# A spectral mixing layer with its dense DFT matmuls replaced by a factored FFT kept in SBUF

## The chip, the cores and the metric

One core of a Trainium2 chip. The metric is the device time of one execution in microseconds (us); where several runs are given, it is their median with the lowest and highest. Runs of one comparison are made on one chip, alternating with the kernel before. Engines: PE is TensorE, PEld its weight loads, DVE is VectorE, ACT is ScalarE, POOL is GpSimd, SP issues the transfers. "Granted clock" is the share of full speed that TensorE was given. The record calls a run slow when it is over 1.5% above the fastest run of the same kernel, and fast otherwise; its verdicts (faster, same or slower by 2%, or unclear) use fast runs alone.

## The reference, cut to what matters

```python
def _A_ref(x, w_r, w_i):                    # x: (1, 2048, 512) bf16
    X = jnp.fft.rfft2(x.astype(jnp.float32), axes=(-2, -1))
    X = X * (w_r + 1j * w_i)                # (2048, 257) spectral weights
    return jnp.fft.irfft2(X, s=(S, D), axes=(-2, -1)).astype(jnp.bfloat16)

h  = x + _A_ref(_layernorm(x), w_r, w_i)
# FFN: 512 -> 1792, squared ReLU, -> 512
r  = jnp.maximum(_layernorm(h) @ w1 + b1, 0)
h2 = h + (r * r) @ w2 + b2
```

## The kernel before

The transforms over rows (2048) and channels (512) are dense matmuls with tables of cosines and sines. They use the fold of row t with row 2048-t, which needs reversed copies of x. Everything is 128-partition bf16, accumulated in PSUM in f32.

```python
for q, (sk, szk) in enumerate(kcols):              # forward transform over rows
    prs = [ps_tile(f"par{db}") for db in range(ND)]
    for c in range(NT):
        for db in range(ND):
            nc.tensor.matmul(prs[db][:, 0:szk], lhsT=xe[:, c, bass.ts(db, P)],
                             rhs=FC[:, c, sk:sk + szk], start=(c == 0), stop=False)
# ... the same with sine tables (pai), then channels (pxr, pxi), z_batch on VectorE,
# ... then the inverse over rows (pcp, psm)

def d2_tile(j):                                    # inverse over channels, residual, statistics
    # ... 4 + 4 matmuls into pyc and pys
    nc.scalar.copy(ysn[:], pys[:, 0:D])
    nc.vector.tensor_tensor(ylo[:], pyc[:, 0:D], ysn[:], ALU.add)
    nc.vector.tensor_tensor(yhi[:], pyc[:, 0:D], ysn[:], ALU.subtract)
    nc.vector.tensor_tensor(xn[:, j, :], xn[:, j, :], ylo[:], ALU.add)
    nc.vector.tensor_tensor(xrv[:, j, :], xrv[:, j, :], yhi[:], ALU.add)
    # ... bn_stats and bn_aggr of both

for g in gorder:                                   # FFN, four groups of 512 rows
    # ... normalise, transpose into UT
    for i in range(NF):                            # NF = 14
        for cd in range(ND):                       # ND = 4
            nc.tensor.matmul(ph[:], lhsT=W1[:, cd, bass.ts(i, P)], rhs=UT[:, g, cd, :], ...)
        nc.scalar.activation(rl[:], ph[:], ACT.Relu, bias=b1f[:, i:i + 1], scale=1.0)
        nc.vector.tensor_tensor(actT[:, i, :], rl[:], rl[:], ALU.mult)
    for ii in range(4):
        for f_i in range(NF):
            nc.tensor.matmul(po[:, 0:D], lhsT=actT[:, f_i, bass.ts(ii, P)], rhs=W2[:, f_i, :], ...)
        nc.tensor.matmul(po[:, 0:D], lhsT=onesrow[0:1, :], rhs=b2b[0:1, :], start=False, stop=True)
        # ... residual, for half of the rows a reversal matmul, store
```

## Time and profile before

| | before |
|---|---|
| time, 3 runs known ahead | 285.85 us (285.51 to 287.39) |
| span of the profiled run | 284.6 us |
| TensorE busy / idle in the span | 232.0 / 52.6 us |
| mean granted clock | 0.94 |

The prediction shows the lines on which it rests. One more view, the span in 40 equal slices of 7.1 us, gives the whole picture of TensorE: the first row is its busy share in tenths, the second the granted clock in tenths.

```profile
PE   0040497999999997999996059999999899999994
...
PEclk9995597989999999999999659999999999999999
```

The 9s from the eighth slice on say that TensorE is nearly always busy and at full clock. The two weak places are the first 35 us and the three slices around 160 us (6, 0, 5).

### The profile page before, as it was taken

The page shows a single profiled execution, that of the slowest core. Times are in us where ns is not written, and L with a number is a line of the kernel's source. Part 1 is how long each engine was busy: PE and PEld are TensorE (multiplying, and loading weights), DVE is VectorE, ACT ScalarE, POOL GpSimd, SP SyncE. Part 2 cuts the span into 40 slices and gives each one's busy share as a digit, 9 for nine tenths or more (in the row PEclk, how much of TensorE's full clock was granted, in tenths as well). Part 3 has the DMA queues.
Part 4 walks back from the last instruction along what each step waited for, and adds up shares of the span by engine and source line. Part 5 has one row for each costly group of instructions (what it writes and reads, how often), then busy time and mean ns, then how long its engine had stood idle before and what let it go on. Part 6 is the DMA issues. An engine that isn't in the chain of part 4 may idle for free.

```text
span 284.6 us, 3080 instructions
## 1 busy us (share of the span) xinstructions
PE 232.0 (81%) x1108; PEld 99.9 (35%) x1108; DVE 140.5 (49%) x317; ACT 131.5 (46%) x205; POOL 49.0 (17%) x62
## 2 busy tenths in 40 slices
PE   0040497999999997999996059999999899999994
PEld 0010133444444443444442034434443444444431
DVE  5278956482301999319909963411531143225310
ACT  1098969967633320232234068702841485048311
POOL 8237699883200000000000000000000000000000
PEclk9995597989999999999999659999999999999999
DMA  5474890000000000000000000011000100110011
GB/s 148 125 184 108 267 277 0 3 0 1 2 0 0 0 3 0 0 0 2 0 0 0 0 0 3 0 37 37 3 0 32 44 0 0 37 39 0 0 37 38
DMA packets 13097, 10.17 MB, mean 36 GB/s; under 512 B 2585, under 2 KB 12570, under 8 KB 13082
## 3 DMA queue, kind: packets, MB, share of 16 engines
q1 hardware_dynamic: 13082, 9.98, 12.1%
q8 instruction: 8, 0.13, 0.2%
q14 instruction: 7, 0.06, 0.1%
HBM read 7.88 MB, written 2.10 MB: 35 GB/s over the span
## 4 chain that ended last, share of the span: by engine, by line
PE 62%; DVE 17%; ACT 9%; POOL 5%; DMA 3%; issue 2%; SPq 1%; DVEq 0%; ACTq 0%
PE ph L444 18%; PE po L453 17%; PE pai L214 5%; PE psm L339 5%; POOL gen_i L20 5%; PE pcp L330 3%; DMA Gx<-in_A_x_dram 3%; DVE gen_m L22 2%; PE po L455 2%; DVE bnst2e L390 2%; PE pyc L371 2%; PE pxr L296 2%; PE pxr L294 2%; ACT xrv L121 1%; PE pys L375 1%
## 5 line engine op out<-in xcount | busy, mean ns | idle before, releaser
L453 PE MATMUL po<-W,actT 128*128 128x512 bf16 x224 | 52.1, 380 | 0.0
L444 PE MATMUL ph<-UT,W 128*128 128x512 bf16 x224 | 50.7, 386 | 0.7 <-ACT UT L439 0.7
L20 POOL TENSOR_SCALAR gen_i<-idx_i,tcols 128x1025 int32<-128x1025 int32 (+1 forms) x30 | 41.9, 1406 | 18.0 <-DVE mv L156 11.9
L448 DVE TENSOR_TENSOR actT<-rl 128x512 bf16<-128x512 bf16 x56 | 23.8, 426 | 34.3 <-ACT rl L447 34.0
L447 ACT ACTIVATE rl<-ph,b1f 128x512 bf16<-128x512 f32 x56 | 36.9, 692 | 8.0 <-PE ph L444 7.8
L196 PE MATMUL par<-FC,xe 128*128 128x512 bf16 (+1 forms) x96 | 18.7, 346 | 17.2 <-DVE xe L172 14.6
L444 PEld LDWEIGHTS <-W 128*128 128x128 bf16 x224 | 22.2, 99 | 28.1 <-issue 3.9
L453 PEld LDWEIGHTS <-actT 128*128 128x128 bf16 x224 | 20.9, 98 | 25.6 <-issue 2.7
L22 DVE TENSOR_SCALAR gen_m<-gen_i 128x1025 int32<-128x1025 int32 (+1 forms) x30 | 19.4, 652 | 13.7 <-POOL gen_i L20 9.4
L439 ACT COPY UT<-putp 128x512 bf16<-128x512 bf16 x16 | 8.2, 598 | 26.6 <-PE putp L438 26.6
L196 PEld LDWEIGHTS <-xe 128*128 128x128 bf16 x96 | 7.8, 104 | 28.8 <-DVE xe L172 15.5
L330 PE MATMUL pcp<-FC,PT 128*128 128x512 bf16 (+1 forms) x72 | 16.7, 379 | 1.2 <-DVE PT L277 1.2
L465 ACT CAST orv<-prout 128x512 bf16<-128x512 f32 x8 | 4.7, 585 | 26.2 <-PE prout L463 22.3
L457 DVE TENSOR_TENSOR ot<-po,xrv 128x512 bf16<-128x512 f32 x8 | 5.5, 692 | 22.2 <-PE po L455 22.2
L457 DVE TENSOR_TENSOR ot<-po,xn 128x512 bf16<-128x512 f32 x8 | 5.5, 692 | 20.9 <-PE po L455 20.9
L214 PE MATMUL pai<-FS,xo 128*128 128x512 bf16 x64 | 15.8, 411 | 0.0
L438 PE MATMUL putp<-ident,u 128*128 128x128 bf16 x64 | 5.3, 242 | 12.5 <-DVE u L429 12.2
L120 PE MATMUL prx<-Gx,Rm 128*128 128x512 bf16 x8 | 3.6, 625 | 14.1 <-DMA Gx<-in_A_x_dram 14.1
L339 PE MATMUL psm<-FS,MT 128*128 128x512 bf16 x64 | 14.3, 379 | 0.0
L332 ACT CAST CPT<-pcp 128x512 bf16<-128x512 f32 x8 | 4.2, 596 | 19.1 <-DVE bufB L262 10.2
L23 ACT ACTIVATE FS<-gen_m,biascol 128x1025 bf16<-128x1025 int32 x9 | 10.2, 1157 | 2.3 <-DVE gen_m L22 2.2
L23 ACT ACTIVATE FC<-gen_m,biascol 128x1025 bf16<-128x1025 int32 x9 | 10.0, 1145 | 2.0 <-DVE gen_m L22 1.9
(141 smaller groups left out, 288.6 us busy)
## 6 DMA issues: line engine op xcount, KB each, us to landing
W<-in_B_w_dram SPq DMA_DIRECT2D x2, 1792.0 KB, 12.5
xn<-in_A_x_dram SPq DMA_DIRECT2D x8, 128.0 KB, 2.3
out_dram<-ot SPq DMA_DIRECT2D x8, 128.0 KB, 1.7
Gx<-in_A_x_dram SPq DMA_DIRECT2D x7, 128.0 KB, 6.3
out_dram<-orv SPq DMA_DIRECT2D x7, 128.0 KB, 2.8
WLr<-in_A_w_r_dram SPq DMA_DIRECT2D x1, 514.0 KB, 3.9
WLi<-in_A_w_i_dram SPq DMA_DIRECT2D x1, 514.0 KB, 5.2
Gw<-in_A_w_r_dram SPq DMA_DIRECT2D x7, 64.2 KB, 3.3
```

Of the source, the lines that this page charges most:

```text
L20: nc.gpsimd.tensor_scalar(fi[:], idx_i_ap, col_f, float(add_const), ALU.mult, ALU.add)
L22: nc.vector.tensor_single_scalar(fm[:], fi[:], period - 1, ALU.bitwise_and)
L23: nc.scalar.activation(out_ap, fm[:], ACT.Sin, bias=biascol, scale=2.0 * np.pi / period * (1.0 - delta))
L196: nc.tensor.matmul(prs[db][:, 0:szk], lhsT=xe[:, c, bass.ts(db, P)], rhs=FC[:, c, sk:sk + szk], start=(c == 0), stop=False)
L214: nc.tensor.matmul(pis[db][:, 0:szk], lhsT=xo[:, c, bass.ts(db, P)], rhs=FS[:, c, sk:sk + szk], start=(c == 0), stop=(c == NT - 1))
L330: nc.tensor.matmul(pcs[b][:, 0:szs], lhsT=lhs, rhs=rhs, start=(c == 0), stop=(c == NT))
L339: nc.tensor.matmul(pms[b][:, 0:szs], lhsT=MT[:, c, bass.ts(b, P)], rhs=FS[:, c, ss:ss + szs], start=(c == 0), stop=(c == NT - 1))
L444: nc.tensor.matmul(ph[:], lhsT=W1[:, cd, bass.ts(i, P)], rhs=UT[:, g, cd, :], start=(cd == 0), stop=(cd == ND - 1))
L447: nc.scalar.activation(rl[:], ph[:], ACT.Relu, bias=b1f[:, i:i + 1], scale=1.0)
L448: nc.vector.tensor_tensor(actT[:, i, :], rl[:], rl[:], ALU.mult)
L453: nc.tensor.matmul(po[:, 0:D], lhsT=actT[:, f_i, bass.ts(ii, P)], rhs=W2[:, f_i, :], start=(f_i == 0), stop=False)
L457: nc.vector.tensor_tensor(ot[:], po[:, 0:D], h_tile(i), ALU.add)
```

## The change

The intent: a radix split of both transforms. Rows are 16 x 128, so a row transform is a small 16-point stage, a twiddle folded into tables, and a 128-point stage. Channels are handled as real 2 x 256. The transform's arithmetic falls from some 464 wide matmuls to about 97,000 columns in small ones, the reversed copies of x go, and what lies between the layer norm and the FFN stays in SBUF. The work is now a loop over eight pairs of row frequencies (stages 2 to 4), then a "prep" of each group of four row blocks (stages 5 and 6, residual, statistics, normalising, transposing) ahead of the FFN ("MLP") of that group. The diff is 824 lines; this is its core.

```diff
-        for q, (sk, szk) in enumerate(kcols):
-            ...                                     # dense row DFT, 8 x 4 matmuls of 512 per chunk
+    for pr in range(8):
+        pu = mm_tile("p2")                          # stage 2: 8 matmuls of 256 columns
+        ...
+        U = fwd.tile([P, 2, 512], BF16, tag="U", bufs=2, name="U")
+        nc.scalar.copy(U[:].rearrange("p q c -> p (q c)"), pu[:])
+        px = mm_tile("p3")                          # stage 3: 4 matmuls of 512
+        ...
+            nc.scalar.copy(AB[:].rearrange("p u r c -> p (u r c)"), px[:])
+            nc.vector.tensor_tensor(Xf[:, 0::3], AB[:, 0], bsw, ALU.add)
+            nc.vector.tensor_tensor(Xf[:, 2:0:-1], AB[:, 0], bsw, ALU.subtract)
+        for m, w in ((mA, WB[0]), (mB, WB[1])):     # spectral weights
+            nc.vector.tensor_tensor(m[:], X[:], w[:, pr]..., ALU.mult)
+        ...                                         # Z (2 instructions), M (2)
+        pt = mm_tile("p4")                          # stage 4: 8 matmuls of 256
+        ...
+        nc.scalar.copy(T2[:, :, :, 2 * pr:2 * pr + 2, :]..., pt[:]...)
@@
+    def prep(c):
+        for g in range(4 * c, 4 * c + 4):
+            ...                                     # stage 5: 4 matmuls of 256 into pe
+            nc.scalar.copy(od[:], pe[:, 256:512])
+            nc.vector.tensor_tensor(R[:, 0:256], pe[:, 0:256], od[:], ALU.add)
+            nc.vector.tensor_tensor(R[:, 256:512], pe[:, 0:256], od[:], ALU.subtract)
+            py = bank("p6")
+            nc.tensor.matmul(py[:], lhsT=KI[:], rhs=R[:], start=True, stop=True)
+            nc.vector.tensor_tensor(hs[:, g, :], py[:], xs[:, g, :], ALU.add)
+            ...                                     # bn_stats, bn_aggr
+            nc.gpsimd.tensor_tensor(hb[:, g, :], hs[:, g, :], b2b[:], ALU.add)
+        nc.gpsimd.tensor_scalar(rs2[:, sl], mv2[:, sl, 1], EPS, None, ALU.add)
+        nc.gpsimd.tensor_tensor(rs2[:, sl], rs2[:, sl], mhalf[:], ALU.pow)
+        ...                                         # normalise, transpose into UT
@@
-                nc.tensor.matmul(po[:, 0:D], lhsT=onesrow[0:1, :], rhs=b2b[0:1, :], start=False, stop=True)
...
+            nc.vector.tensor_tensor(ot[:], po[:], hb[:, g, :], ALU.add)
@@
+    prep(0)
+    prep(1)
+    mlp(0)
+    prep(2)
+    mlp(1)
+    prep(3)
+    mlp(2)
+    mlp(3)
```

## The prediction

> **What bounds the kernel now.** I read the page's first part, then the table of stretches, then the chain in order of time, then the groups of instructions for unit costs.
>
> ```profile
> PE 232.0 (81%) x1108; PEld 99.9 (35%) x1108; DVE 140.5 (49%) x317; ACT 131.5 (46%) x205; POOL 49.0 (17%) x62
> ```
>
> TensorE is busy for 232 of 284.6 us. The stretches (start:end, length, busy us and count of PE, PEld, DVE, ACT, POOL, granted clock, DMA share, GB/s) show where:
>
> ```profile
> 14.00:35.00 21.00, 6.22 (x15) 2.03 (x16) 17.54 (x47) 19.48 (x26) 11.37 (x7) 0.68 0.65 178
> 60.00:93.00 33.00, 32.35 (x152) 14.51 (x150) 9.54 (x25) 17.16 (x34) 6.98 (x10) 1.00 0.00 1
> 160.00:168.00 8.00, 1.41 (x12) 1.00 (x13) 7.45 (x23) 1.88 (x4) 0.00 (x0) 0.50 0.00 0
> 175.00:284.60 109.60, 104.38 (x500) 44.93 (x498) 33.64 (x69) 47.04 (x76) 0.00 (x0) 1.00 0.06 20
> ```
>
> To 35 us layer norm and sine tables run and PE waits. From there to 154 us PE is dense in the DFT matmuls. From 154 to 168 us VectorE finishes the statistics with PE idle at half clock. Then comes the FFN. The chain agrees: layer norm, tables, matmuls, a VectorE tail, then the FFN alone (start us, us, what):
>
> ```profile
> 27.84 1.36 DVE un L166 x2
> ...
> 55.63 15.06 PE pai L214 x61
> ...
> 139.98 7.03 PE psm L339 x32
> ...
> 164.43 0.23 DVE mv L391 x2
> ...
> 169.07 13.57 PE ph L444 x56
> 182.64 3.02 PE po L453 x14
> 185.66 0.32 PE po L455
> ```
>
> So the time is 164.4 us of transform, 4.6 us to the first FFN matmul, 111 us of FFN and 4.5 us of tail. One warm FFN matmul of 512 columns costs 50.7/224 = 0.226 us. The unit costs that I use:
>
> ```profile
> L378 ACT COPY ysn<-pys 128x512 f32<-128x512 f32 x8 | 4.7, 585 | 10.0 <-PE pys L375 4.7 <-DVE yhi L382 3.6 <-DVE bnst2e L390 1.2
> L173 DVE TENSOR_TENSOR xo<-un,urv 128x512 bf16<-128x512 bf16 x8 | 3.3, 407 | 0.0
> L272 DVE TENSOR_TENSOR bufA<-bufA,tmp 128x1028 bf16<-128x1028 bf16 x1 | 0.7, 701 | 0.0
> L381 DVE TENSOR_TENSOR ylo<-pyc,ysn 128x512 f32<-128x512 f32 x8 | 5.3, 663 | 8.6 <-ACT ysn L378 8.6
> L390 DVE BATCH_NORM_STATS2 bnst2e<-xn 128x6 f32<-128x512 bf16 x8 | 5.5, 683 | 0.0
> L20 POOL TENSOR_SCALAR gen_i<-idx_i,tcols 128x1025 int32<-128x1025 int32 x18 | 31.1, 1739 | 15.8 <-DVE mv L156 11.9 <-DVE gen_m L22 3.4
> ```
>
> Handoffs between engines take about 0.03 us in the chain. Independent VectorE instructions in a row start about 0.09 us before the one ahead ends; dependent ones do not.
>
> **What the Trainium skill says.** "TensorE: Matmul & The Clock Gate", Part 1, has TensorE at half clock after an idle window of about 3.4 us, and at full clock only after a busy one. The trace agrees: PE stops at 154.1, the clock falls to 0.50 at 158.2, and it returns at 171.9, 2.8 us into dense matmuls. One 1.9 us hole at 42.4 was enough for half clock from 45.5. The same page, Part 3, "What overlaps and what doesn't", has matmuls strictly first in, first out. This decides the change; no line of this trace contradicts it. "ScalarE: Activation LUTs", "What ACT_TABLE_LOAD costs", gives 186 ns + 0.833 ns an element: 613 ns for 512, measured 585, so I take 1.02 us for 1024 elements. "GPSIMD Engine Reference", 3.1, gives about 2.6 cycles at 1.2 GHz an element for two-input work: an estimate of 1.1 us for the new 512-wide residual add there. No trace line has one.
>
> **The change, part by part.** *Arithmetic.* The dense DFT groups (about 464 matmuls of 512 columns, with the reversals and edge columns about 130 us of PE busy time) go. In their place are, by counting columns, 64x256 (row stage), 28x128 (transposes), 14x256 (weight reversal), 8 pairs of 16x256 + 4x512, and 16 rows of 4x256 + 512: 97,000 columns. At 512 columns in 0.216 us they are 41 us, at half clock 82. If PE still set the end, about 90 us would go. But in the built order PE's queue is serial: stage 4 of pair k stands before stage 2 of pair k+1 for every pair but the first, and each "prep" group stands whole between two MLP groups. PE thus waits through every other engine's work.
>
> *Prologue, estimate 38.5 us.* x comes in four transfers; the first lands about 3.7. Layer norm needs 16 x (0.70 + 0.41 to 0.49) on VectorE, about 20 us with set-up. But each chunk's rstd is made on GpSimd, behind tables and weight scaling in its queue: two scalings of 2048 elements at 1.1 ns (undisturbed) to 1.7 ns (the row above) = 2.3 to 3.5 us each, also waiting for the spectral weights' DMA, and a 1152-wide table ahead of the last chunk. I work the last chunk out at 27.5. ScalarE then has that chunk's two copies (2 x 1.02) and the last E sine (1.25): 32.5. Transposes need all three E kinds, 28 x 0.12 = 3.4, then the reversal matmuls 14 x 0.213 = 3.0 at half clock: 38.9, say 38.5.
>
> *Pair loop, 83 us.* One period is: stage 4 and the next stage 2, 15 x 0.213 + 0.40 = 3.6; U copy 1.02; stage 3, 3 x 0.427 + 0.61 = 1.9; copy 1.02; VectorE 0.32 + 0.41 + 0.60 + 0.69 + 0.32 + 0.41 + 0.32 + 0.41 = 3.5; handoffs 0.15. That is 11.2 us at half clock and 9.0 at full. VectorE's 3.5 with its copy leaves PE idle over 4.5 us per period, more than a clock window, so I expect mostly half clock: 10.6. Seven periods 74, the first pair 11, less the missing last stage 2 and the hoisted part of pair 1 (3), plus the last copy 1: 83. The small real-channel fixes on GpSimd lie beside four stage-4 matmuls that do not need them.
>
> *Preps, 60 us.* One row block runs stage 5, 3 x 0.213 + 0.40 = 1.04; od copy 0.37; sum and difference from PSUM (half of 0.663's slope) 0.79 with an aggregate between; stage 6, 0.61; then the residual and statistics beside the next stage 5. That is 2.9 us per block cold and 2.7 warm. A group of four is 1.4 + 3 x 2.9 + 3.0 = 13.1, then rstd on GpSimd 0.8, normalising 1.5, and transposes 1.1 to 1.4. Two groups before the first MLP are 30; the other two, each exposed between MLPs, 15 each.
>
> *FFN, 104 us.* 4 x 112 x 0.2225 = 99.7. The bias matmul (0.32 x 16 = 5.1 us on the chain) and the reversal (8 x 0.38) are gone. Three cold starts add about 2 us each, less three early matmuls each: +4. Tail: 0.7 + a store of about 2.3 = 3.
>
> Sum: 38.5 + 83 + 60 + 104 + 3 = 288.5 of span, 289.7 with the 1.2 us by which timed runs exceed the profiled span (285.85 against 284.6). So 90 us of matmul saved come back as serial latency.
>
> **Rivals.** (1) PE stays the bound and the saving shows: 41 us of transform in place of 130, the tables smaller: about 200 us. For it: PE is 81% busy now. Against: the strict queue order, 4.5 us of other engines per pair. (2) The clock stays up in loop and preps: 1.6 less per pair and 0.2 per block give about 275. For it: stages 4 and 2 run back to back for 3.6 us, nearly a window; against: the one 1.9 us hole in the trace already cost the clock. (3) GpSimd sets the prologue: if its strided bf16 scaling or its power function runs at several times the 1.1 ns per element, the prologue becomes 45 to 50 and the total 297 to 300; no trace line has such work. (4) VectorE sets the loop: no, it has 28 us of 83.
>
> **Range and chances.** Prologue +-4, loop -14 to +7, preps -6 to +4, FFN +-2. The loop and prep errors lean towards shorter, since I took nearly cold PE and no overlap that the order does not show. I therefore place the point below the sum, at 284 us, with 268 to 299. Half of the mass is within 2% (280.1 to 291.6) or near it: faster 0.38, same 0.41, slower 0.21.
>
> **What would show it.** Right: PE busy near 60%, granted clock 0.5 to 0.65 between 40 and 150 us; eight equal periods of 10 to 11.5 us in the chain, with VectorE 3.5 of each; PE holes of some 10 us before the third and fourth MLP group; the first FFN matmul that is followed densely near 150 us. Wrong: stage 2 of pair k+1 running during VectorE's part of pair k, periods under 9 us, the prologue past 45 us, or preps hidden beside MLP matmuls.

## The result, and the profile after

| | before | after |
|---|---|---|
| time, 4 runs each, same chip | 286.53 us (285.51 to 287.39) | 294.00 us (293.55 to 294.48) |
| ratio | | 1.0249, 95% interval 1.0206 to 1.0293 |
| span of the profiled run | 284.6 us | 292.4 us |
| TensorE busy / idle | 232.0 / 52.6 us | 180.6 / 111.8 us |
| mean granted clock | 0.94 | 0.784 |

A ratio here is over fast runs alone, and not quite the ratio of the medians. The kernel became 2.5% slower, and the table says how: TensorE lost 51 us of busy time and gained 59 us of idle time.

The first part of the page of the kernel after, engines with busy time, share and count:

```profile
PE 180.6 (62%) x858; PEld 93.2 (32%) x872; DVE 128.3 (44%) x299; ACT 93.0 (32%) x123; POOL 56.7 (19%) x109
```

No engine is near full. The table of stretches of the kernel after, columns as in the prediction, cut near the first loop matmuls (they start at 41.1), at the end of the loop, and each change between prep and dense FFN matmuls:

```profile
0.00:41.50 41.50, 19.16 (x112) 12.75 (x113) 25.68 (x68) 16.43 (x17) 22.67 (x49) 0.88 0.57 194
41.50:125.10 83.60, 35.92 (x168) 20.50 (x168) 27.68 (x63) 25.98 (x27) 10.69 (x36) 0.65 0.00 0
125.10:159.20 34.10, 15.79 (x75) 8.93 (x77) 20.05 (x48) 5.26 (x11) 11.71 (x12) 0.55 0.00 1
159.20:182.80 23.60, 23.49 (x110) 10.77 (x110) 8.03 (x17) 10.66 (x16) 0.00 (x0) 1.00 0.05 17
182.80:200.20 17.40, 7.59 (x39) 4.01 (x39) 10.71 (x25) 1.89 (x5) 5.83 (x6) 0.61 0.03 8
```

TensorE idles 22.3 us of the prologue, 47.7 us of the loop (83.6 less 35.9), 37.7 us of the preps (18.3 here, 9.8 here, 9.6 in the last one). The FFN stretches, here one of four, have none. The last three are 23.5, 23.5 and 24.2 us, the last prep 17.5 and the tail 3.5. In the dense stretch TensorE runs at full clock; in loop and preps at 0.55 to 0.65.

One period of the loop, from the chain in order of time of the kernel after (start us, us, what):

```profile
86.68 1.02 ACT AB L277
87.72 0.43 DVE X L282
88.52 0.69 DVE mA L288
89.21 0.61 DVE mB L288
89.84 0.43 DVE Z L290
90.73 0.44 DVE M L300
93.23 1.39 PE p L251 x8
94.70 1.02 ACT U L254
96.96 1.02 ACT AB L277
```

From one AB copy to the next is 10.28 us. The work passes from engine to engine, each waiting for the one before, so none is busy for half of it. (Shorter pieces fall out of this list of the longest and fill its gaps: the second X, Z and M, stage 4's eight matmuls from 91.2 to 93.2, and stage 3's four from 95.8.) What TensorE waits for stands in its groups (line, engine, what, shape, count, busy us, mean ns, idle us before and its releaser); the third line is for the prologue:

```profile
L316 PE MATMUL p<-EI,M 128*128 128x256 bf16 x28 | 11.6, 414 | 32.8 <-DVE M L300 32.8
L366 PE MATMUL p<-R,KI 128*128 128x512 bf16 x16 | 8.9, 556 | 22.0 <-DVE R L364 22.0
L160 DVE TENSOR_SCALAR un<-xs,mv,rs 128x512 bf16<-128x512 bf16 x16 | 11.1, 742 | 4.7 <-POOL rs L158 4.7
```

Stage 4 waited 32.8 us for VectorE's M, 4.7 us in each of seven pairs. Stage 6 waited 22.0 us for R in the preps. In the prologue, VectorE's normalising took 742 ns in the mean, with single ones from 396 to 2055 ns, the long ones beside GpSimd instructions. The Trainium skill, "SBUF — State Buffer", "Who interferes with whom", has VectorE and GpSimd share a port pair as an exclusive lock: when VectorE works in a mode that uses two ports, which its `tensor_scalar` can enter, the second to issue blocks until the first is done. This trace agrees in kind: two of them, from 14.49 us on, took 2.31 us together beside a GpSimd scaling that ran from 14.71 to 16.66. No run shows which mode they were in.

How a prep ends, from the timeline of the kernel after (start us, us, engine, line, what):

```profile
138.35 0.18 DVE L370 BATCH_NORM_AGGREGATE mv<-st 128x2 f32<-128x6 f32 x1
138.91 0.23 POOL L373 TENSOR_SCALAR rs<-mv 128x4 f32<-128x4 f32 x1
139.22 1.04 POOL L374 TENSOR_TENSOR rs<-rs,mhalf 128x4 f32<-128x4 f32 x1
140.30 1.38 DVE L378 TENSOR_SCALAR u<-hs,mv,rs 128x512 bf16<-128x512 bf16 x4 [1.77 <-POOL rs L374]
```

The last statistics end at 138.53 and normalising starts at 140.30: 1.77 us for four reciprocal roots. The add first waits for the last residual add (hb) in GpSimd's queue, and the power of four numbers takes 1.04 us.

### The profile page after: what moved, and what is told of

Its sections match the earlier page's. It is cut to its first block, busy times and chain, and to the rows that moved or that the text cites. A ratio compares the mean times of both kernels' runs of the same rounds, so it can differ in the third digit from the quotient of the medians.

```text
span 292.4 us, 2459 instructions
## 1 busy us (share of the span) xinstructions
PE 180.6 (62%) x858; PEld 93.2 (32%) x872; DVE 128.3 (44%) x299; ACT 93.0 (32%) x123; POOL 56.7 (19%) x109
## 4 chain that ended last, share of the span: by engine, by line
PE 54%; DVE 26%; ACT 8%; POOL 5%; issue 3%; DMA 1%; POOLq 0%; ACTq 0%; DVEq 0%
PE ph L395 17%; PE po L403 16%; DVE hs L367 4%; PE p L251 3%; PE p L366 3%; DVE st L369 3%; DVE un L160 3%; ACT U L254 3%; DVE st L154 3%; PE p L385 3%; PE p L316 2%; ACT AB L277 2%; PE p L317 2%; DVE mA L288 2%; DVE R L363 2%
## 5 line engine op out<-in xcount | busy, mean ns | idle before, releaser
L403 PE MATMUL po<-W,act 128*128 128x512 bf16 x220 | 48.8, 379 | 0.2
L398 DVE TENSOR_TENSOR act<-rl 128x512 bf16<-128x512 bf16 x56 | 23.8, 425 | 33.0 <-ACT rl L397 33.0
L371 POOL TENSOR_TENSOR hb<-hs,b2b 128x512 f32<-128x512 bf16 x16 | 18.4, 1150 | 91.2 <-DVE hs L367 84.5
L316 PE MATMUL p<-EI,M 128*128 128x256 bf16 x28 | 11.6, 414 | 32.8 <-DVE M L300 32.8
L403 PEld LDWEIGHTS <-act 128*128 128x128 bf16 x224 | 22.0, 98 | 26.4
L405 DVE TENSOR_TENSOR ot<-po,hb 128x512 bf16<-128x512 f32 x16 | 11.1, 692 | 35.5 <-PE po L403 35.5
L170 PE MATMUL p<-KF,un 128*128 128x256 bf16 x32 | 12.5, 395 | 20.1 <-DVE KF L127 14.2
L318 ACT CAST T<-p 128x1024 bf16<-128x1024 f32 x8 | 8.1, 1012 | 44.2 <-PE p L317 39.1
L367 DVE TENSOR_TENSOR hs<-p,xs 128x512 bf16<-128x512 f32 x16 | 11.1, 692 | 10.4 <-PE p L366 10.4
L358 PE MATMUL p<-GI,T 128*128 128x256 bf16 x64 | 14.8, 373 | 1.1 <-ACT T L318 1.1
L386 ACT COPY UT<-p 128x1024 bf16<-128x1024 bf16 x8 | 7.7, 1015 | 24.2 <-PE p L385 24.2
L251 PE MATMUL p<-GF,Bt 128*128 128x256 bf16 x64 | 13.1, 370 | 0.0
```

What stands on the lines that cost most here:

```text
L251: nc.tensor.matmul(puv[:, q, :, e, :], lhsT=Bt[:, 2 * t + e, 2 * pr + q, :], rhs=GFv[:, t, :, e, :], start=(t == 0), stop=(t == 1))
L316: nc.tensor.matmul(o, lhsT=M[:, 0, r, c0:c0 + P], rhs=ei[:, P:3 * P], start=True, stop=False)
L358: nc.tensor.matmul(pe[:, 256 * e:256 * e + 256], lhsT=T2[:, lt, g].rearrange("p q s -> p (q s)"), rhs=GI[:, lt, :], start=(r == 0), stop=( ...
L367: nc.vector.tensor_tensor(hs[:, g, :], py[:], xs[:, g, :], ALU.add)
L371: nc.gpsimd.tensor_tensor(hb[:, g, :], hs[:, g, :], b2b[:], ALU.add)
L398: nc.vector.tensor_tensor(act[:, f, :], rl[:], rl[:], ALU.mult)
```

## The experiments

The theory: the time is set by the order in TensorE's queue. Stage 2 and 3 of the next pair stand behind stage 4 of this one, which waits for VectorE; and each prep stands whole between two MLPs. Rivals: the half clock sets it; or GpSimd's work does (reciprocal roots, weight scaling). All kernels gave correct results. Line numbers in an experiment's profile are those of its own source. The kernel before was measured in each comparison: 287.63 us with e1 to e4 (e2b and e2c apart), 287.87 with e2b, e2c, e5 and e6, 286.22 with e0, e7 and e8.

### e0_control: the kernel after, again

> The changed kernel itself, unedited, as a control on the chip of this job. Every theory expects 292.5 to 294.5 us and a span near 292.4; if it lies 1.5 us or more from 294.0, the small differences of the rstd and weight-scaling experiments are to be read against the new value.

Measured: 292.26 us (291.93 to 293.12), ratio 1.0207, interval 1.015 to 1.0263. So the kernel after lies between 292 and 294 us by job, and an edit's gain of 1 to 2 us can't be read from comparisons of different jobs. This weakens e4 and e5 below. The profiles show where such a difference sits: the loop ended at 125.1 us in the kernel after and at 122.9 in the control, its clock 0.65 and 0.69. In the profiles of e3, e4, e5 and e7, whose edits leave the loop alone, it ended at 123.9, 124.4, 124.8 and 124.1.

### e1_loop_order: the loop's stages issued ahead

```diff
-    for pr in range(8):                 # p2(k), p3(k), rest(k)
+    st2(0)
+    st2(1)
+    st3(0)
+    for pr in range(8):
+        if pr < 6:
+            st2(pr + 2)
+        if pr < 7:
+            st3(pr + 1)
+        st4(pr)
```

> Same arithmetic as the changed kernel; only the pair loop is emitted in another order, so that in TensorE's queue stages 2 of pair k+2 and 3 of pair k+1 stand before stage 4 of pair k. Theory A (the serial queue order sets the loop): the period falls from 10.35 us to 4 to 5 (VectorE's 3.5 plus gaps), the loop from 83.6 to about 43, the total from 294 to 250 to 258. Rival B (the period is the engines' own latency and half clock, not the order): PE at half clock has 5.4 us of work and 1 to 2 of waits a period, so about 7 us, total 268 to 275. Rival C (VectorE or PSUM buffers keep it serial anyway): within 2% of 294.

Measured: 252.72 us (248.47 to 253.29). One run was over 1.5% faster than the others, so those three count as slow; the gain, 41 us by the median and 46 by the one fast run, is far outside that. The stretch of the loop in its profile, which is of a slow run (253.29):

```profile
41.50:82.10 40.60, 26.05 (x172) 15.56 (x170) 27.27 (x63) 25.03 (x27) 11.06 (x36) 0.90 0.00 1
```

The same instructions on VectorE (27.3 us) and ScalarE (25.0 us) now overlap: the loop is 40.6 us instead of 83.6, its period 4.3 us in the mean instead of 10.4, and TensorE's clock is 0.90. The order was the cause, and the clock came back with the density; e2b below parts the two.

### e2_clock_fill and e2b_clock_fill_pinned: full clock in the old order

```diff
         pt = mm_tile("p4")
+        for _ in range(14):
+            nc.tensor.matmul(pt[:, 0:512], lhsT=KI[:], rhs=GF[:, 0, :], start=True, stop=True)
```

The fillers keep TensorE busy in the hole ahead of stage 4; their result is overwritten.

> The changed kernel with 14 idle matmuls of 512 columns ahead of each stage 4, into the PSUM tile that stage 4 then overwrites: 3.0 us at full clock, inside VectorE's 4.5 us hole. The result stays right. Theory A (half clock is one term of the loop, about 1.2 us of each 10.35): granted clock in the loop near 1.0, period 9.0 to 9.3, total 284 to 287. Rival B (most of the period is half clock): period under 8, total under 276. Rival C (the clock costs nothing, or the fill delays stage 4): 293 or more.

Measured: 272.2 us (270.6 to 273.35), ratio 0.9477 (0.9417 to 0.9538). That is rival B's number (under 276, a period of 7.1 us in the mean), but not for the clock alone: with the fillers the scheduler had also put stage 2 of the next pair (L251) ahead of stage 4 (L318), as its timeline shows:

```profile
83.69 1.04 PE L251 MATMUL p<-GF,Bt 128*128 128x256 bf16 x8
...
85.55 0.28 PE L318 MATMUL p<-EI,M 128*128 128x256 bf16 x1 [0.82 <-DVE M L300]
```

The run is confounded, and taken alone it would have blamed the clock for what the order did. e2b pins stage 2 behind stage 4 again:

```diff
+        with (tc.issue_after(last.ins) if last is not None else nullcontext()):
             for q in range(2):          # stage 2 as before
```

> The run before with idle matmuls was confounded: the scheduler also moved stage 2 of pair k+1 ahead of stage 4 of pair k. Here the idle matmuls stay and the order is pinned to that of the changed kernel. Theory A (clock alone is worth about 1.2 us of 10.35 a period): granted clock near 1.0 in the loop, period 9.0 to 9.3, total 284 to 287. Rival B (the clock gave most of the 22 us): total under 277.

Measured: 284.49 us (282.52 to 286.05), ratio 0.9907 (0.9836 to 0.9979). Its loop, cut where its last T copy ends:

```profile
41.50:113.50 72.00, 47.76 (x270) 25.36 (x275) 27.68 (x63) 24.50 (x26) 10.70 (x36) 1.00 0.00 1
```

At full clock the loop is 72.0 us from the same start, 11.6 less than 83.6, and its period 9.0 instead of 10.4. The whole run is 9.5 us shorter than the 294.0, and 7.8 than the control. So the lost clock costs some 8 to 12 us of the loop; the order costs the rest.

### e2c_stage2_early: one stage ahead, no fillers

```diff
+    st2(0)
+    for pr in range(8):
+        st3(pr)
+        if pr < 7:
+            st2(pr + 1)
+        st4(pr)
```

> The other half of the confounded run: stage 2 of pair k+1 ahead of stage 4 of pair k, without idle matmuls. Theory A (order alone takes stage 2 and its copy, 1.7 + 1.02, off the path, with the clock still near half): period about 8.0, total 276 to 280. Rival B (it was the clock): total over 285.

Measured: 278.81 us (278.62 to 279.68), ratio 0.9719 (0.9663 to 0.9774). Its loop, cut in the same way:

```profile
41.50:107.50 66.00, 35.28 (x161) 19.52 (x163) 27.67 (x63) 24.65 (x26) 10.71 (x36) 0.73 0.00 0
```

Putting stage 2 and its copy beside VectorE's work takes 17.6 us off the loop and 15 off the whole; the period is 8.1 us. e1, which also puts stage 3 there, takes 43 us off the loop. It also explains e2: early stage 2 and a full clock together gave a loop of 60.1 us (it ended at 101.6).

### e3_prep_inside: preps issued between the MLP's matmuls

```diff
-    def prep(c):
+    def prep_steps(c):                  # the same body, cut into pieces by "yield"
...
     def mlp(c):
+        nxt = prep_steps(c + 1) if c < 3 else iter(())
         ...
             nc.vector.tensor_tensor(act[:, f, :], rl[:], rl[:], ALU.mult)
+            next(nxt, None)
```

> The changed kernel with the row-block preparation of groups 1 to 3 emitted in small pieces between the matmul groups of the MLP before it; nothing else moved. Theory A (the preparation costs because it stands whole in TensorE's queue): three stretches of 17.4, 17.4 and about 16 us shrink to their matmul work of about 3.6 us each, total 250 to 258. Rival B (ScalarE and VectorE are too full beside an MLP, so that its own relu and square chain is delayed): less than half of that, total over 274.

Measured: 264.08 us (263.19 to 264.98), ratio 0.9199 (0.9146 to 0.9251), 6 us above the range. The first prep, still alone, and 28 us of the MLPs with a prep inside:

```profile
125.00:142.00 17.00, 7.15 (x33) 3.56 (x32) 10.02 (x24) 2.11 (x5) 5.88 (x6) 0.50 0.00 0
...
170.00:198.00 28.00, 26.19 (x140) 12.34 (x138) 17.23 (x42) 12.58 (x20) 5.99 (x6) 1.00 0.04 15
```

TensorE is busy 26.2 of 28 us. The kernel gained 30 us (294.0 less 264.1), so three preps that took some 52 us alone take some 22 inside the MLPs. What went is the preps' serial wait. The miss is in what stays: from 142.0 to 258.4 us TensorE is busy for 110.5 us and idle for 5.9, where the four MLPs alone have 94.3 and 0.5. So each prep adds some 5.4 us of busy time, where the expectation had 3.6, and the idle time adds 5.4 in all. Why the busy time is larger was not followed up.

### e4_rstd_scalar: the reciprocal root of a prep off GpSimd

```diff
-        nc.gpsimd.tensor_scalar(rs2[:, sl], mv2[:, sl, 1], EPS, None, ALU.add)
-        nc.gpsimd.tensor_tensor(rs2[:, sl], rs2[:, sl], mhalf[:], ALU.pow)
+        nc.scalar.activation(rs2[:, sl], mv2[:, sl, 1], ACT.Sqrt, bias=epsc[:], scale=1.0)
+        nc.vector.reciprocal(rs2[:, sl], rs2[:, sl])
```

> The changed kernel with the second layer norm's reciprocal square root taken off GpSimd: square root on ScalarE, reciprocal on VectorE. Theory A (the term of 0.8 us that the prediction gave to rstd is 1.77 us in the trace, all on the path, because GpSimd's power takes 1.04 us and stands behind its residual add): 1.77 falls to about 0.6 in each of four groups, total down by 4 to 5.5 us, 288.5 to 290. Rival B (something else releases the normalising at the same time): less than 1.5 us.

Measured: 292.4 us (291.78 to 293.5), ratio 1.0187 (1.012 to 1.0254): a miss for theory A; rival B, a gain under 1.5 us, is nearer. From its timeline:

```profile
137.64 0.18 DVE L372 BATCH_NORM_AGGREGATE mv<-st 128x2 f32<-128x6 f32 x1
...
138.41 1.38 DVE L380 TENSOR_SCALAR u<-hs,mv,rs 128x512 bf16<-128x512 bf16 x4
...
140.60 1.93 ACT L388 COPY UT<-p 128x1024 bf16<-128x1024 bf16 x2 [2.44 <-PE p L387]
...
142.41 0.39 ACT L363 COPY od<-p 128x256 f32<-128x256 f32 x1
```

The wait itself fell from 1.77 to 0.59 us as expected. But between the first two preps nothing was gained: the order of ScalarE's queue changed too, and the od copy of the second prep now waits behind both UT copies. The inner preps went from 17.4 to 16.4 us. What a change to one wait is worth depends on what stands next.

### e5_weights_on_scalar: GpSimd's weight scaling moved to ScalarE

```diff
-        nc.gpsimd.tensor_scalar(dst[:, 0:8, 0], src[:, 0:8], WSC, 1.0, ALU.mult, ALU.mult)
+        nc.scalar.activation(dst[:, 0:8, 0], src[:, 0:8], ACT.Copy, scale=WSC)
```

> The changed kernel with the scaling of the spectral weights moved from GpSimd to ScalarE, nothing else. In the changed kernel the four normalisings of a chunk take 1.38 us alone and 2.4 to 3.5 us beside a GpSimd instruction, and rstd stands behind the scalings. Theory A (both cost on the path): the start of the E transposes moves from 36.5 to about 33, total down 2.5 to 4.5 us, 289.5 to 291.5. Rival B (ScalarE's queue or the third E table takes its place): within 1 us of 294.

Measured: 292.59 us (291.15 to 293.57), ratio 1.0176 (1.0101 to 1.0252): between the theories. The group of the normalising:

```profile
L160 DVE TENSOR_SCALAR un<-xs,mv,rs 128x512 bf16<-128x512 bf16 x16 | 7.8, 542 | 5.2 <-POOL rs L158 5.2
```

Each normalising instruction took 200 ns less, 3.3 us in all, when GpSimd had less to do beside it. But the transposes that end the prologue started only 0.9 us earlier (35.58 instead of 36.46). The chains of the two runs say why: the last chunk's copies on ScalarE ended at 33.41 instead of 35.34, but two sines of the E table, and not one, then stood behind them in ScalarE's queue, until 35.53. So 1.9 us were won ahead of ScalarE, and some 1.0 of them lost to the order in its queue, as rival B has it. Against the control's 292.26 the total shows no gain.

### e7_prep_fill: full clock in the preps

```diff
             py = bank("p6")
+            for _ in range(6):
+                nc.tensor.matmul(py[:], lhsT=KI[:], rhs=GI[:, 0:2, :]..., start=True, stop=True)
```

> Six idle 512-column matmuls ahead of stage 6 of every row block, in TensorE's hole of 1.4 us there, to keep the clock up; the order is otherwise unchanged. Theory A (the preps are a serial chain; the half clock is a small part of it: stage 6 is 0.58 and four stage 5 matmuls 1.06 us in each 2.81 us row block, and the transposes with the first matmuls of the MLP some 2.5 us a group): at full clock 0.3 to 0.6 us less per row block for 16 blocks and about 1.5 less per group, minus about 1.5 us per group for fillers that run at half clock at its start: 284 to 291 us. Rival (the preps' length is set by the half clock): row blocks of about 2 us, total 272 to 280. Rival (the waits on VectorE and ScalarE alone count): 293 to 296, no gain.

Measured: 292.9 us (290.91 to 294.1), ratio 1.0212, against 292.26 for the control on the same chip: no gain in the total, a miss for theory A; the third forecast (waits alone, 293 to 296) is nearest. The stage 6 group of its profile:

```profile
L368 PE MATMUL p<-R,KI 128*128 128x512 bf16 x16 | 6.3, 393 | 3.4 <-DVE R L364 3.4
```

The clock did come back (393 instead of 556 ns), and three row blocks of the first group took 6.95 us instead of the control's 8.44. Most of it was spent again: the first fillers of each group run at half clock in front of stage 6, and the first two preps together take 33.9 us with and without fillers. The inner preps got 1.5 and 1.3 us shorter, and the MLPs behind them 0.7 and 0.9 longer. That leaves 1.2 us, which the total doesn't show because the loop, untouched, ended 1.2 us later than in the control. So fillers are no lever in the preps. That the clock itself is worth nothing there isn't shown: the warm row blocks were 0.5 us shorter each.

### e8_bias_on_pe: the bias matmul put back

```diff
-            nc.gpsimd.tensor_tensor(hb[:, g, :], hs[:, g, :], b2b[:], ALU.add)
...
+            nc.tensor.matmul(po[:], lhsT=ones[0:1, :], rhs=b2b[0:1, :], start=False, stop=True)
-            nc.vector.tensor_tensor(ot[:], po[:], hb[:, g, :], ALU.add)
+            nc.vector.tensor_tensor(ot[:], po[:], hs[:, g, :], ALU.add)
```

> The second bias goes back into each output tile as a one-row matmul, as in the kernel before, and the residual add on GpSimd goes. Theory A (TensorE sets the end in the MLPs, so each of 16 bias matmuls counts in full at 0.22 to 0.32 us: +3.5 to +5.1; and rstd no longer waits for the last residual add: -0.4 us in each of four groups): 295.5 to 298 us. Rival (the bias matmul was hidden and costs nothing; only rstd's start moves): 291.5 to 293.

Measured: 302.1 us (300.85 to 303.59), ratio 1.0542 (1.048 to 1.0603), 9.8 us over the control. The start times on TensorE:

```profile
214.59 3.19 PE L403 MATMUL po<-W,act 128*128 128x512 bf16 x14
217.71 0.39 PE L404 MATMUL po<-b2b,ones 1*128 1x512 bf16 x1
218.03 3.19 PE L403 MATMUL po<-W,act 128*128 128x512 bf16 x14
```

From one row block to the next is 3.44 us, of which 14 matmuls at 0.2157 are 3.02. A one-row bias matmul therefore costs 0.42 us, not the 0.22 to 0.32 of the expectation, and 16 of them 6.7 us. The kernel before has the same spacing (182.48, 185.91, 189.36). The other 3 us can't be put down to the bias: the last loop copy ended at 125.9 in this run and at 122.9 in the control, and the edit touches nothing there; under e0 that end moved between 122.9 and 125.1 with no edit to the loop. In the two profiles the difference is 11.6 us: 3.0 to the loop's end, 6.7 of bias, and 1.9 that I did not follow up.

### e6_all: e1, e3, e4 and e5 together

> Loop order, preparation inside the MLP, rstd on ScalarE and VectorE, and weights on ScalarE together. If the losses add (41 + 30 + 2 + 3): 294 - 76 = 218, range 213 to 225, and faster than both kernels. If they hide one another: 230 or more.

Measured: 216.16 us (213.88 to 216.47), ratio 0.7513 (0.7457 to 0.757): 25% faster than the kernel before, and in the expected range. The page's first part and 30 us of the MLPs with a prep inside:

```profile
PE 162.0 (75%) x858; PEld 84.1 (39%) x872; DVE 122.7 (57%) x304; ACT 98.5 (46%) x132; POOL 48.1 (22%) x97
```

```profile
128.00:158.00 30.00, 29.34 (x152) 13.89 (x154) 17.98 (x43) 12.88 (x21) 4.72 (x4) 1.00 0.07 23
```

TensorE has the same 858 instructions recorded as in the kernel after, and is busy for 162.0 instead of 180.6 us with them at a higher clock (0.897 in the mean, where it was 0.784). The gain, 78 us, is 7 more than e1's and e3's together; e4 and e5 alone showed none that stands clear of the spread, so how the 7 divide stays open. The saving that the change was made for is there once the order lets it show.

## Why the prediction was right or wrong, point by point

**The class was wrong.** I called "within 2%" the likeliest; it was 2.5% slower. The time, 294.0, lies in the range.

**The mechanism was right, and shown.** The prediction said that TensorE waits through every other engine's work because its queue is serial. Its signs came: TensorE busy for 62%, a clock of 0.65 and 0.55, VectorE's 3.5 us in each period; and none of its signs of being wrong. Two signs were off: the holes of some 10 us stand before the second and third MLP group, not the third and fourth, and the first dense FFN matmul came at 159.1, not near 150. e1, e2c and e3 change the order and little else, and take 41, 15 and 30 us away. So the strict order was where the expected gain went. Rival 1, "about 200 us", is what a better order nearly reaches: 216.

**Pair loop, 83 us: right.** Measured 83.6. The period was 10.25 to 10.6, 10.35 in the mean, against 10.6, and 9.0 at full clock in e2b, as worked out. The mixture was a little different: stage 4 ran at half clock, but stage 3's matmuls stood 0.21 us apart, at full clock. The first pair took about 11.4 us from its first matmul to its T copy's end, some 2 more than the sum has for it, which used up what the periods gave.

**Preps 60 and FFN 104: right as a sum, wrong apart.** Measured 69.0 (34.1 + 17.4 + 17.5) and 94.8 (23.6 + 23.5 + 23.5 + 24.2), together 163.8 against 164. The preps' own terms, 13.1 + 0.8 + 1.5 + 1.1 to 1.4, make 16.5 to 16.8 per group, and I wrote 15: 6 to 7 us dropped in rounding. The root on GpSimd was 1.77, not 0.8, 1 us more in each group. On the other side, an FFN matmul took 0.2157 us, not 0.2225 (448 x 0.007 = 3 us), and the cold starts that I put into the FFN fell into the preps, where the transposes and the first MLP matmuls run at half clock. The two errors cancelled by luck.

**Prologue 38.5: too short by 3.** The first x chunk landed at 4.96, not 3.7, and normalising beside GpSimd took up to 2.06 us for one instruction where I used 0.41 to 0.49. The last chunk, which I had at 27.5, was normalised at 32.8, 5.3 us late; its reciprocal root and its normalising stood behind and beside GpSimd's tables. The next term was too long instead: 27.5 + 2 x 1.02 + 1.25 is 30.8, and I wrote 32.5, which hid 1.7 us of the miss. e5 shows that the slow normalising is real, and that only 0.9 us of it comes back if the weight scaling leaves. How the rest divides stays open.

**The steps that failed: the lean at the end, and the prologue's last chunk.** The sum was 289.7 and the result 294.0, 1.5% apart: 3.0 for the prologue, 0.9 for loop, preps, FFN and tail together, 0.4 for the difference between time and span (1.6, not 1.2). But I then put the point at 284, because "the loop and prep errors lean towards shorter, since I took nearly cold PE and no overlap that the order does not show". That was 5.7 of the 10 us of error. The runs show no such lean: loop and preps came out 0.6 and 9.0 us longer than their terms. The order built was the order run, so no overlap came; and the clock was 0.65 in the loop and 0.55 in the preps, which the prediction itself names as a sign of being right. A warm loop would have been 11.6 us shorter (e2b), but that is Rival 2, and in numbers the lean stood for over a third of it (289.7 to 284, where Rival 2 has 275). Taken unshaded, the sum would still have said +1.4%, inside the 2% class; the prologue's 3 us carried the result over it.

**The removed side.** I priced the bias at 5.1 us. e8 shows 6.7 for the matmuls alone: each costs 0.42 us in start-to-start time, where I had taken its 0.32 in the chain. The sum was built from the new kernel's own parts, so this did not enter it.

## What to carry to other kernels

Before counting on saved matmuls, write down what TensorE's queue has next while another engine works on this iteration; if the answer is "the consumer of that work", the saving comes back as waiting, and look first at issuing the next iteration's stages earlier: here that was worth 41 us, and neither edit to a single wait (e4, e5) more than 2. When a bottom-up sum from measured durations stands, do not move the point away from it by a feeling about the sign of its errors: check the addends again instead, here 15 against 16.6. The clock penalty came with the waiting, so remove the waiting first; fillers in the old order bought 8 to 12 us in the loop and about 1 us behind it. Check what the scheduler made of an edit before reading its time: e2 was not the experiment that it was meant to be. And read a stretch only up to where its own last instruction ends.

## What the Trainium skill lacked or had wrong

- "GPSIMD Engine Reference" has no cost for the power function: 1.04 us for 128x4 numbers, where an add of the same size took 0.23 us. What the prediction worked out from its section 3.1 for a two-input add (about 2.6 cycles an element at 1.2 GHz; an estimate of 1.1 us for 512 columns) agrees with the 1.15 us measured.
- "TensorE: Matmul & The Clock Gate" gives an idle and a busy window, but not how busy or how idle a window must be to count: in the kernel before, one hole of 1.93 us (to 44.29) was followed by half clock from 45.5 us; in the kernel after, from 127.83 to 136.28 us, TensorE was busy 4.31 of 8.45 us with no hole over 1.4 us, and was granted 0.50 throughout; the loop, with a hole of 4.7 us in each period of 10.3 us, was granted 0.65.
- The same page has no start-to-start cost for a one-row matmul among 128-row ones: 0.42 us of TensorE's time for 512 columns, against 0.216 us for a full one.
- "SBUF — State Buffer" describes the lock between VectorE and GpSimd without a measured case of normalising: a 512-wide one took from 0.40 us to, beside GpSimd, 2.06 us, and the mean of the 16 fell from 742 to 542 ns when GpSimd had less to do.
